# GpSimd's selection masks ahead of its wait for the tiny loads, P.V of quad 5 among the keys of quad 7, the first 24 heads turned ahead of the last maxima

## The chip, the cores and the metric

The kernel runs on one core of a Trainium2 chip. The metric is the device time of one launch in microseconds (us). Before the change the median of three runs is 202.33 us (201.74 to 202.46).

Five engines work beside each other, each with a queue of its own that is worked off in order: TensorE (PE in the profile; PEld is its weight load), VectorE (DVE), ScalarE (ACT), GpSimd (POOL) and SyncE (SP, which here only issues transfers). They meet at semaphores: an engine that reaches a wait stands until the count is there, and all that is behind it in its queue stands too.

## The reference

One token goes through two branches that are mixed by a gate. Cut to what matters:

```python
q = (x @ wq).reshape(32 heads, 128)
scores = q . k_cache * 128**-0.5          # 32 heads x 4096 keys x 128
p = softmax(scores)
a = (p . v_cache).reshape(4096) @ wo      # wo: 4096 x 512
h = relu(x @ w1 + b1); b = (h * h) @ w2 + b2
g = sigmoid(sum(x * gate_w))
out = g * a + (1 - g) * b                 # 512 values
```

The two caches are 32 MB each in bf16; with the weights the core reads some 78 MB.

## The kernel before

**Quads.** The 32 heads are worked through in 8 quads of 4 (`R = 4`, `NQ = 8`). The keys of a quad are 4 MB, laid as 128 partitions (4 heads x 32 rows) by 128 blocks of 128 elements; the values likewise. The SBUF tensor `KV` has four slots of 4 MB. SP issues the loads in the order K0, K1, V0, K2, V1, K3, V2, K4, V3, K5, V4, K6, K7, V5, V6, V7; from the fifth on, a load waits until what was in its slot is used up (`done`: for keys the products of DVE, `s_sd`, and the transposes of PE, `s_t`; for values `s_pv`). V7 comes in four parts of 1 MB. Behind V7 SP issues, once the last keys are used up, the last rows of `wo` (`wob`, L322, into the slot of K7) and most of `w2` (L307, L309).

**Scores.** Of the 128 blocks of a quad DVE takes 64 (16 in each quarter): one `tensor_tensor_reduce` a block (`ttr`, L702), which multiplies keys by the broadcast query `qb` and sums into a column of `S`. PE takes the other 64 in 8 groups of 8: it transposes a group (`transposes`, L480), ACT copies it from PSUM to `kT` (`evac`, L404), and PE multiplies it by the query column (`scores`, L492). In PE's queue the scores of a group stand two groups behind its transposes. After the eighth group ACT copies the scores to `S` (`s_copy`, L410).

**Softmax of a quad, done while the keys of the next one pass.** DVE takes the maximum over `S` (`smax`, L710, column of `mp`); PE turns it to a row (`max_rows`, L502) behind group 2 of the next quad; DVE reduces it to the four heads (`gmax`, L714 and L717, the row `dg`), behind the first 16 products of that quad; PE spreads it over the partitions (`max_cols`, L506) behind group 4; ACT copies it (`nM`, L414) and takes the exponentials with their sums (`exps`, L422) behind its fifth copy of a group. PE then sums over partitions (`den`, L514), multiplies by the values (`pv`, L525, 128 small matmuls), and DVE divides (`recip`, L724; `norm`, L730, which writes `onorm` and applies the gate). For quads 0 to 4 `den` and `pv` come at the end of the next quad's keys. Those of quad 5 come behind the last scores of quad 7, and after them the end of the kernel.

**The end.** PE's queue after the last scores: `den(5)`, `pv(5)`, `max_rows(7)`, `turn_a` (transposes `onorm` of heads 0 to 23, L545), `max_cols(7)`, `spread_a` (L552), `out_a` (L563, 128 matmuls with the rows of `wo` for the first 23 heads and more), `den(6)`, `pv(6)`, part of `w2`, `den(7)`, `pv(7)`, `regroup` for the last 8 heads (L569, L572), `out_b` (L581), the rest of `w2`, and the output.

**The selection masks.** `spread_a` puts the 24 heads' results into the order in which the rows of `wo` lie in SBUF, by a matmul with a 0/1 matrix (`selA`); `regroup` does so with `selB`. GpSimd makes both in the memory of `w1_sb`, once `mlp_h` (the first MLP matmuls, behind quad 2) has read `w1`: one memset (L363), one `affine_select` for `selB` (L365) and 19 for `selA` (L371, a count on `s_sb` after each, and each waits for the one before). Ahead of this GpSimd issues 14 transfers of rows of `wo` (L356) and 9 tiny transfers into unused memory (L353), which move the order of its DMA rings on; it waits for those 9 (L361, `s_dm`), then for `mlp_h` (`s_h`), and then makes the masks.

Of the kernel before, what the change touches and what calls it, by code (L numbers as in the profile page):

```python
# [5 lines left out]
def bass_gated_mix__gqa_block_cached__dense_activation_squared_relu__decode_kernel(  # L6
# [31 lines left out]
    R = 4  # L38
    NQ = NH // R
# [73 lines left out]
    with ctx:  # L113
# [90 lines left out]
        s_dm = [sem(f"s_dm{n}") for n in range(len(RUNS))]  # L204
# [22 lines left out]
        s_cp = sem("s_cp")  # L227
# [5 lines left out]
        s_nm = sem("s_nm")  # L233
# [3 lines left out]
        s_rd = sem("s_rd")  # L237
# [94 lines left out]
        @block.gpsimd  # L332
        def _(eng):
            eng.memset(ident[:, :], 0.0).then_inc(s_id, 1)
            eng.memset(identf[:, :], 0.0).then_inc(s_id, 1)
            eng.memset(onesf[:, :], 1.0).then_inc(s_cst, 1)
            eng.wait_ge(s_id, 2)
            for m in (ident, identf):
                eng.affine_select(out=m[:, :], in_=m[:, :], compare_op=ALU.not_equal, fill=1.0,
                                  base=0, pattern=[[-1, 128]], channel_multiplier=1)\  # L340
                   .then_inc(s_id, 1)
            eng.memset(E[:, :, :, :], 0.0).then_inc(s_ze, 1)
            eng.memset(RS[:, :], 0.0).then_inc(s_ze, 1)
            eng.memset(hd[:, :, :], 0.0).then_inc(s_ze, 1)
            eng.wait_ge(s_qps, NQ)
            q = 0
            sent = 0
            for n, ((back, d), run) in enumerate(zip(turns(), RUNS)):
                if back:
                    eng.inc_swdge_sem([], [], mode="reset_dge_cursor")  # L350
                if d:
                    src = B_w1[0:d, 0:32].rearrange("p (a c) -> p a c", a=2)
                    eng.dma_start(dm[0:d, sent, :, 0:8], src[:, :, 0:8]).then_inc(s_dm[sent], 16)  # L353
                    sent += 1
                p, st, k = place(*run)
                eng.dma_start(W[p:p + st * (k - 1) + 1:st, :], woa_v[q:q + k, :],  # L356
                              max_dma_last_dim=8192).then_inc(s_wp[n], 16)
                q += k
            assert q == STRIPS[len(RUNS)][3] and STRIPS[-1][3] + STRIPS[-1][2] == 4 * HX
            for n in range(sent):  # L360
                eng.wait_ge(s_dm[n], 16)  # L361
            eng.wait_ge(s_h, 1)
            eng.memset(w1_sb[0:NA, 0:3, 0:1024], 0.0).then_inc(s_sb, 1)  # L363
            eng.wait_ge(s_sb, 1)
            eng.affine_select(out=selB, in_=selB, compare_op=ALU.not_equal, fill=1.0,  # L365
                              base=0, pattern=[[8, 2], [1, 8], [-1, 128]], channel_multiplier=16)\
               .then_inc(s_sb, 1)
            for n, (p, st, k, q) in enumerate(STRIPS):
                eng.wait_ge(s_sb, n + 2)
                part = selA[:, :, p:p + st * (k - 1) + 1]  # L370
                eng.affine_select(out=part, in_=part, compare_op=ALU.not_equal, fill=1.0, base=-st * q,  # L371
                                  pattern=[[st, 4], [-1, st * (k - 1) + 1]], channel_multiplier=4 * st)\
                   .then_inc(s_sb, 1)

# [71 lines left out]
        def _(eng):  # L448
# [34 lines left out]
            def scores(q, g):  # L483
                n = GQ * q + g
                if g == 0:
                    eng.wait_ge(s_qc, q + 1)
                    if q >= 2:
                        eng.wait_ge(s_cp, R * (q - 1))
                eng.wait_ge(s_ev, n + 1)
                for y in range(GB):  # L490
                    c = GB * g + y
                    mm = eng.matmul(pS[q % 2][:, R * c:R * c + R], kT[:, n % NT, y * 128:(y + 1) * 128],  # L492
                                    qcol[:, R * q:R * q + R], start=True, stop=True)
                mm.then_inc(s_s2, 1)

            def max_rows(q):
                eng.wait_ge(s_mp, q + 1)
                if q >= 1:
                    eng.wait_ge(s_nm, q)
                if q >= 1:  # L500
                    eng.wait_ge(s_rd, q if q < NQ - 2 else q - 1)
                eng.transpose(MT, mp[:, q:q + 1], identf[:, :]).then_inc(s_mt, 1)  # L502

            def max_cols(q):
                eng.wait_ge(s_dg, q + 1)
                eng.matmul(MB[:, q:q + 1], dg[:, q % 2, :], onesf[0:1, 0:1],  # L506
                           start=True, stop=True).then_inc(s_mb, 1)

            def den(q):
                eng.wait_ge(s_e, R * (q + 1))  # L510
                eng.wait_ge(s_nm, q + 1 if q < NQ - 3 else min(q + 2, NQ))
                if q == NQ - 1:
                    eng.wait_ge(s_rd, q)
                eng.matmul(DEN[:, R * q:R * q + R], onesf[:, :], RS[:, R * q:R * q + R],  # L514
                           start=True, stop=True).then_inc(s_den, 1)

            def pv(q):
                if q >= 1:
                    eng.wait_ge(s_on, q)
                else:  # L520
                    eng.wait_ge(s_bg, 1)
                for j in range(NP):
                    eng.wait_ge(s_v[q][part_of(V_PARTS[q], j)], 16)
                    for b in range(PB * j, PB * j + PB):
                        mm = eng.matmul(O[:, R * q:R * q + R], KV[:, V_SLOT[q], b * 128:(b + 1) * 128],  # L525
                                        E[:, q % NE, COLUMN[b], :], start=(b == 0), stop=(b == NB - 1))
                mm.then_inc(s_pv, 1)
# [14 lines left out]
            def turn_a():  # L542
                eng.wait_ge(s_on, NA // R)
                eng.wait_ge(s_ev, GQ * NQ)
                eng.transpose(KP[2][0:NA, 0:128], onorm[:, 0:NA], ident[:, :]).then_inc(s_at, 1)  # L545

            def spread_a():
                eng.wait_ge(s_ac, 1)
                eng.wait_ge(s_cp, R * NQ)
                eng.wait_ge(s_sb, 2 + len(STRIPS))  # L550
                for c in range(4):
                    mm = eng.matmul(O2A, selA[:, c, :], oA[:, 32 * c:32 * c + 32],  # L552
                                    start=(c == 0), stop=(c == 3))
                mm.then_inc(s_at, 1)
# [63 lines left out]
            for q in range(NQ):  # L618
                for g in range(GQ):
                    transposes(q, g)  # L620
                    if g >= 2:
                        scores(q, g - 2)
                    for c, (a, b) in Q_AT.items():
                        if (a, b) == (q, g):
                            q_rows(c)
                        if (a, b + 2) == (q, g):
                            q_cols(c)
                    if g == 2 and q >= 1:
                        max_rows(q - 1)
                    if g == 4 and q >= 1:  # L630
                        max_cols(q - 1)
                scores(q, GQ - 2)
                scores(q, GQ - 1)
                if q == 0:
                    eng.wait_ge(s_b, 32)
                    eng.wait_ge(s_ez, 1)
                    eng.transpose(B2, b2r, ident[0:4, 0:4]).then_inc(s_b2, 1)
                if 1 <= q < NQ - 2:
                    den(q - 1)
                    pv(q - 1)  # L640
                if q == 2:
                    mlp_h()
            den(NQ - 3)
            pv(NQ - 3)
            max_rows(NQ - 1)
            turn_a()
            max_cols(NQ - 1)
            spread_a()
            eng.wait_ge(s_hs, 2)
# [19 lines left out]
        def _(eng):  # L669
# [82 lines left out]
            for q in range(NQ):  # L752
                for j in range(NP):
                    ttr(q, j)
                    if j == 0 and q == 1:
                        bias()
                    if j == 0 and q >= 1:
                        gmax(q - 1)
                    if j == 1 and 2 <= q < NQ - 1:
                        norm(q - 2)  # L760
                    if j == 1 and q == 4:
                        mlp()
                if q == NQ - 1:
                    recip(q - 2)
                    norm(q - 2)
                smax(q)
                if 1 <= q < NQ - 2:
                    recip(q - 1)
            gmax(NQ - 1)
            eng.wait_ge(s_at, 1)  # L770
            eng.tensor_copy(oA[:, :], KP[2][0:NA, 0:128]).then_inc(s_ac, 1)
            eng.wait_ge(s_at, 2)
            eng.tensor_copy(o2A[:, :], O2A).then_inc(s_ac, 1)
            for q in (NQ - 2, NQ - 1):
# [42 lines left out]
```

## Time and profile before

| | us |
|---|---|
| median of 3 runs | 202.33 (201.74 to 202.46) |
| the profiled execution | 202.62 |
| its span, first to last instruction | 201.3 |
| PE busy | 124.3 |
| DVE busy | 124.0 |
| ACT busy | 98.9 |
| GpSimd (POOL) busy | 37.7 |
| HBM read, 78.32 MB, over the span | 389 GB/s |
| mean granted PE clock | 0.674 of full |

In the page's 40 slices the DMA engines are busy at 9 tenths or more from the second slice to the 37th, and nearly idle in the last three. Busy times are shares of the whole span: an engine that waits for keys in the middle may still be the one that everything waits for at the end. Lines such as L525 are those of the kernel before.

### The profile page before, as it was taken

The page shows a single profiled execution, that of the slowest core. Times are in us where ns is not written, and L with a number is a line of the kernel's source. Part 1 is how long each engine was busy: PE and PEld are TensorE (multiplying, and loading weights), DVE is VectorE, ACT ScalarE, POOL GpSimd, SP SyncE. Part 2 cuts the span into 40 slices and gives each one's busy share as a digit, 9 for nine tenths or more (in the row PEclk, how much of TensorE's full clock was granted, in tenths as well). Part 3 has the DMA queues.
Part 4 walks back from the last instruction along what each step waited for, and adds up shares of the span by engine and source line. Part 5 has one row for each costly group of instructions (what it writes and reads, how often), then busy time and mean ns, then how long its engine had stood idle before and what let it go on. Part 6 is the DMA issues. An engine that isn't in the chain of part 4 may idle for free.

```text
span 201.3 us, 6499 instructions
## 1 busy us (share of the span) xinstructions
PE 124.3 (62%) x2420; PEld 111.2 (55%) x2422; DVE 124.0 (62%) x1086; ACT 98.9 (49%) x212; POOL 37.7 (19%) x56
## 2 busy tenths in 40 slices
PE   0039576982639298857279455925492825839686
PEld 0013365762639297846179355925492725829685
DVE  1100599999239950899079925993499999820011
ACT  3007489898119910695058803980298908340000
POOL 5000000069900000000000000000001979960000
PEclk9999799695557955695555555795579765555555
DMA  6999999999999999999999999999999999999300
GB/s 241 483 423 417 417 425 433 462 395 445 402 433 410 427 445 425 445 420 405 435 420 420 440 438 415 420 427 422 432 423 422 430 427 401 408 418 392 100 3 3
DMA packets 5659, 78.74 MB, mean 391 GB/s; under 512 B 1705, under 2 KB 2187, under 8 KB 2444
## 3 DMA queue, kind: packets, MB, share of 16 engines
q1 hardware_dynamic: 4078, 75.76, 88.7%
q0 software_dynamic: 1536, 2.56, 3.4%
q8 instruction: 19, 0.31, 0.6%
q14 instruction: 12, 0.10, 0.1%
q10 hardware_dynamic: 14, 0.01, 0.0%
HBM read 78.32 MB, written 0.00 MB: 389 GB/s over the span
## 4 chain that ended last, share of the span: by engine, by line
another core or an unknown queue 49%; POOL 17%; PE 11%; DMA 11%; ACT 5%; issue 4%; DVE 1%; POOLq 1%; SPq 0%; DVEq 0%; ACTq 0%
DMA KV<-in_A_k_cache_dram 11%; POOL w_sb L371 9%; POOL W L356 4%; PE pO L525 3%; ACT kT L404 3%; POOL xb L353 3%; PE pQ L462 3%; PE pQ L563 2%; ACT qb L393 2%; POOL w_sb L363 1%; POOL w_sb L365 1%; PE KP L480 1%; PE pQ L581 1%; PE pQ L597 0%
## 5 line engine op out<-in xcount | busy, mean ns | idle before, releaser
L702 DVE CUSTOM_DVE_ANT_0 KV<-KV,qb 128x128 bf16<-128x128 bf16 x512 | 113.1, 285 | 32.8 <-DMA KV<-in_A_k_cache_dram 32.8
L404 ACT ACTIVATE kT<-KP 128x1024 bf16<-128x1024 bf16 x64 | 62.1, 1026 | 55.3 <-PE KP L480 54.0
L480 PE MATMUL KP<-ident,KV 128*128 128x128 bf16 x512 | 51.8, 271 | 21.1 <-DMA KV<-in_A_k_cache_dram 21.1
L480 PEld LDWEIGHTS KP<-ident,KV 128*128 128x128 bf16 x512 | 42.9, 124 | 23.7 <-DMA KV<-in_A_k_cache_dram 20.1
L492 PE MATMUL pS<-qcol,kT 128*128 128x4 bf16 x512 | 23.6, 168 | 26.9 <-ACT kT L404 26.5
L702 DVE DVE_READ_ACCUMULATOR2_ANT S<- 128x1 f32 x512 | 38.4, 75 | 0.0
L492 PEld LDWEIGHTS pS<-qcol,kT 128*128 128x128 bf16 x512 | 21.0, 104 | 29.7 <-ACT kT L404 29.3
L525 PEld LDWEIGHTS pO<-E,KV 128*128 128x128 bf16 x1024 | 29.5, 105 | 1.8 <-issue 1.8
L525 PE MATMUL pO<-E,KV 128*128 128x4 bf16 x1024 | 28.6, 166 | 1.7 <-issue 1.7
L363 POOL MEMSET w_sb<- 24x3072 bf16 x1 | 2.6, 2647 | 100.0 <-DMA xb<-in_B_w_dram 100.0
L422 ACT ACTIVATE E<-S,nM 32x128 bf16<-32x128 f32 x32 | 18.4, 575 | 0.9
L371 POOL TENSOR_SCALAR_AFFINE_SELECT w_sb<-w_sb 24x36 bf16<-24x36 bf16 (+5 forms) x19 | 17.3, 910 | 3.1 <-POOL w_sb L371 0.5
L462 PE MATMUL pQ<-W,xb 128*128 128x512 bf16 x18 | 7.1, 530 | 12.3 <-DMA W<-in_A_wq_dram 10.9
L353 POOL DMA_DIRECT2D xb<-in_B_w_dram x9 | 5.3, 590 | 38.8 <-PE pQ L462 38.8
L393 ACT ACTIVATE qb<-pQ 32x128 bf16<-32x128 f32 x20 | 5.4, 268 | 13.0 <-PE pQ L462 12.6
L462 PEld LDWEIGHTS pQ<-W,xb 128*128 128x128 bf16 x20 | 2.0, 117 | 14.3 <-DMA W<-in_A_wq_dram 10.9
L410 ACT ACTIVATE S<-pS 32x64 f32<-32x64 f32 x32 | 6.9, 215 | 4.3 <-PE pS L492 3.7
L683 DVE TENSOR_SCALAR e<-ez 128x1 f32<-128x1 f32 x1 | 0.2, 154 | 12.8 <-ACT ez L431 12.8
L422 ACT ACTIVATION_READ_ACCUMULATOR E<-S,nM 32x1 f32 x32 | 8.0, 249 | 0.0
L356 POOL DMA_DIRECT2D W<-in_A_wo_dram x14 | 7.8, 562 | 0.0
L730 DVE SCALAR_TENSOR_TENSOR onorm<-pO,gcol,rden 128x4 bf16<-128x4 f32 x8 | 1.7, 211 | 9.8 <-PE pO L525 9.8
L506 PE MATMUL pM<-onesf,dg 1*128 1x1 f32 x16 | 3.6, 294 | 5.3 <-DVE dg L717 5.3
(86 smaller groups left out, 78.5 us busy)
## 6 DMA issues: line engine op xcount, KB each, us to landing
KV<-in_A_k_cache_dram SPq DMA_DIRECT2D x8, 4096.0 KB, 28.2
KV<-in_A_v_cache_dram SPq DMA_DIRECT2D x7, 4096.0 KB, 37.0
W<-in_A_wq_dram SPq DMA_DIRECT2D x1, 4096.0 KB, 12.5
KV<-in_A_v_cache_dram SPq DMA_DIRECT2D x4, 1024.0 KB, 21.8
W<-in_A_wo_dram POOLq DMA_DIRECT2D x2, 768.0 KB, 26.5
w_sb<-in_B_w_dram SPq DMA_DIRECT2D x1, 1376.0 KB, 11.6
w2a<-in_B_w_dram SPq DMA_DIRECT2D x2, 512.0 KB, 23.5
KV<-in_A_wo_dram SPq DMA_DIRECT2D x1, 1024.0 KB, 11.3
```

The source lines that it names most:

```text
L353: eng.dma_start(dm[0:d, sent, :, 0:8], src[:, :, 0:8]).then_inc(s_dm[sent], 16)
L356: eng.dma_start(W[p:p + st * (k - 1) + 1:st, :], woa_v[q:q + k, :], max_dma_last_dim=8192).then_inc(s_wp[n], 16)
L371: eng.affine_select(out=part, in_=part, compare_op=ALU.not_equal, fill=1.0, base=-st * q, pattern=[[st, 4], [-1, st * (k - 1) + 1]], chann ...
L393: eng.activation(qb[rows(r), c, :], QR[c][rows(r), r * 128:(r + 1) * 128], ACT.Copy)\
L404: eng.activation(kT[:, n % NT, :], KP[n % 3][:, :], ACT.Copy).then_inc(s_ev, 1)
L410: eng.activation(S[rows(r), q % NS, 0:YQ], S2[rows(r), :, r], ACT.Copy).then_inc(s_cp, 1)
L422: eng.activation(E[rows(r), q % NE, :, r], S[rows(r), q % NS, :], ACT.Exp, bias=nM[rows(r), q:q + 1], scale=SCALE, accum_out=RS[rows(r), h ...
L462: mm = eng.matmul(QR[c], xb[:, t, :], wq_sb[:, t, c * 512:(c + 1) * 512], start=(t == 0), stop=(t == 3))
L480: mm = eng.transpose(KP[n % 3][:, y * 128:(y + 1) * 128], key(q, b), ident[:, :])
L492: mm = eng.matmul(pS[q % 2][:, R * c:R * c + R], kT[:, n % NT, y * 128:(y + 1) * 128], qcol[:, R * q:R * q + R], start=True, stop=True)
L525: mm = eng.matmul(O[:, R * q:R * q + R], KV[:, V_SLOT[q], b * 128:(b + 1) * 128], E[:, q % NE, COLUMN[b], :], start=(b == 0), stop=(b == N ...
L702: ins = eng.tensor_tensor_reduce(key(q, b), key(q, b), qb[:, q, :], 1.0, 0.0, ALU.mult, ALU.add, S[:, q % NS, c:c + 1])
```

## The change

GpSimd's waits for the 9 tiny transfers move behind the masks. `den(5)` moves to the end of quad 6's keys, `pv(5)` behind group 4 and `max_cols(6)` of quad 7's keys; DVE's `recip(5)` follows `smax(6)`, and `norm(5)` follows the third quarter of quad 7's products. `turn_a` comes right behind the last scores, ahead of `max_rows(7)`; DVE's copy `oA` comes ahead of `gmax(7)`. Some waits are adapted: `max_rows(6)` now waits for `recip(5)`; `den(5)` no longer waits for `nM` of quad 6; `spread_a` waits for the score copies of quads 0 to 6 in place of all eight.

```diff
--- before.py
+++ after.py
@@ -357,8 +357,6 @@
             assert q == STRIPS[len(RUNS)][3] and STRIPS[-1][3] + STRIPS[-1][2] == 4 * HX
-            for n in range(sent):
-                eng.wait_ge(s_dm[n], 16)
             eng.wait_ge(s_h, 1)
             eng.memset(w1_sb[0:NA, 0:3, 0:1024], 0.0).then_inc(s_sb, 1)
             eng.wait_ge(s_sb, 1)
@@ -371,6 +369,8 @@
                                   pattern=[[st, 4], [-1, st * (k - 1) + 1]], channel_multiplier=4 * st)\
                    .then_inc(s_sb, 1)
+            for n in range(sent):
+                eng.wait_ge(s_dm[n], 16)
@@ -498,7 +498,7 @@  (max_rows)
                 if q >= 1:
-                    eng.wait_ge(s_rd, q if q < NQ - 2 else q - 1)
+                    eng.wait_ge(s_rd, q if q < NQ - 1 else q - 1)
@@ -508,7 +508,7 @@
             def den(q):
                 eng.wait_ge(s_e, R * (q + 1))
-                eng.wait_ge(s_nm, q + 1 if q < NQ - 3 else min(q + 2, NQ))
+                eng.wait_ge(s_nm, q + 1 if q < NQ - 2 else min(q + 2, NQ))
@@ -546,7 +546,7 @@
             def spread_a():
                 eng.wait_ge(s_ac, 1)
-                eng.wait_ge(s_cp, R * NQ)
+                eng.wait_ge(s_cp, R * (NQ - 1))
@@ -629,21 +629,22 @@
                     if g == 4 and q >= 1:
                         max_cols(q - 1)
+                    if g == 4 and q == NQ - 1:
+                        pv(q - 2)
                 scores(q, GQ - 2)
                 scores(q, GQ - 1)
...
+                if 1 <= q < NQ - 1:
+                    den(q - 1)
                 if 1 <= q < NQ - 2:
-                    den(q - 1)
                     pv(q - 1)
                 if q == 2:
                     mlp_h()
-            den(NQ - 3)
-            pv(NQ - 3)
+            turn_a()
             max_rows(NQ - 1)
-            turn_a()
             max_cols(NQ - 1)
             spread_a()
@@ -760,15 +761,14 @@
                     if j == 1 and q == 4:
                         mlp()
-                if q == NQ - 1:
-                    recip(q - 2)
-                    norm(q - 2)
+                    if j == 2 and q == NQ - 1:
+                        norm(q - 2)
                 smax(q)
-                if 1 <= q < NQ - 2:
+                if 1 <= q < NQ - 1:
                     recip(q - 1)
-            gmax(NQ - 1)
             eng.wait_ge(s_at, 1)
             eng.tensor_copy(oA[:, :], KP[2][0:NA, 0:128]).then_inc(s_ac, 1)
+            gmax(NQ - 1)
             eng.wait_ge(s_at, 2)
             eng.tensor_copy(o2A[:, :], O2A).then_inc(s_ac, 1)
```

## The prediction

> **What bounds the kernel now.** I read the chain of work that ended last first, then the waits, the timelines of PE and DVE from 155 us on, the landings of the loads, and the DMA queues.
>
> The chain from 155 us runs through GpSimd's mask building and then through PE alone (columns: start us, us, what).
>
> ```profile
> 155.11 2.66 POOL w_sb L363
> ...
> 165.06 10.16 POOL w_sb L371
> ...
> 179.67 0.24 POOL w_sb L371
> ...
> 180.42 0.28 PE pS L552 x4
> 180.72 0.20 DVE o2A L773
> ...
> 181.29 3.55 PE pQ L563 x128
> 184.84 0.43 PE pM L514 x2
> 185.27 0.69 PE pO L525 x26
> 185.96 1.75 issue
> 187.71 2.88 PE pO L525 x102
> 190.59 0.43 PE pQ L597 x16
> 191.02 0.43 PE pM L514 x2
> 191.44 3.45 PE pO L525 x128
> ```
>
> So from 180.42 to the end the span is PE's own queue, and `spread_a` (L552) starts when the last mask is there. The waits say how long each side stood (total us, times, longest us).
>
> ```profile
> POOL w_sb L363 <- DMA xb<-in_B_w_dram: 100.0, 1, 100.0
> ...
> PE pS L552 <- POOL w_sb L371: 1.9, 1, 1.9
> ```
>
> In the timeline PE, in quad 7, first stands for DVE's `dg` (`max_cols(6)`), and after P.V of quad 5 for `mp` of the last quad.
>
> ```profile
> 164.99 0.58 PE L506 MATMUL pM<-onesf,dg 1*128 1x1 f32 x2 [4.91 <-DVE dg L717]
> 165.50 1.03 PE L480 MATMUL KP<-ident,KV 128*128 128x128 bf16 x8
> ...
> 176.96 0.37 PE L502 MATMUL pM<-identf,mp 128*1 128x128 f32 x1 [0.57 <-DVE mp L710]
> ```
>
> DVE's time in quad 7 in two stretches (stretch, length, busy and records; then clock, DMA share, GB/s): 16 key products beside GpSimd, then 48 products and two small operations while GpSimd stood in one 10.16 us instruction.
>
> ```profile
> 158.03:164.41 6.38, 6.38 (x32) 0.77 0.99 420
> 164.41:175.10 10.69, 10.66 (x101) 0.50 0.96 405
> ```
>
> The second stretch gives 0.2125 us a product. DMA: the values of quad 5 were issued at 137.2 and took 25.8 us.
>
> ```profile
> L278 SPq DMA_DIRECT2D KV<-in_A_v_cache_dram x1: 328/328/328, 137.2 to 137.2; - x1
> ...
> DMA to landing us min/median/max: 25.8/25.8/25.8
> ```
>
> They land at 163.0. The same answer for the other large loads gives K6 143.5, K7 153.2, V6 172.7, V7's four parts 176.4 to 183.9, and for the last weights 186.5 (`wob`) to 189.0.
>
> **The 1.75 us of "issue"** is PE without instructions. Queue 8 carries 19 packets of 0.31 MB in all, 16 KB or 256 instructions of 64 bytes each (an estimate from PE's 4955 records of all kinds). The halts at 77.20 and 187.71 lie a multiple of 256 records apart. A packet of the next-but-one block starts 2.1 to 4.7 us (mean 3.2) after PE crosses a block's end while the load queue is full, 1.1 once it is empty. It lasts 1.07 and is usable some 1.4 later (186.30 to 187.71). A loaded block thus takes 5.6 us, while 128 small matmuls with their weight loads use one up in 3.6. The window from crossing to halt's end, and the code packet in 185 to 186.5 and in 188.7 to 190.1:
>
> ```profile
> 182.04:187.70 5.66, 3.92 (x134) 3.84 (x130) 0.18 (x1) 0.00 (x0) 0.00 (x0) 0.50 0.95 355
> ...
> q8 instruction: 1, 0.02, 4.9%
> ...
> q8 instruction: 1, 0.02, 5.4%
> ```
>
> **The change, part by part.**
>
> *Masks before the wait.* GpSimd now waits only for `mlp_h` (L538's last matmul, 80.3), so its 24.9 us (155.1 to 180.0) start near 80.5, beside quads 3 and 4. Price there: in quad 7 the contact cost DVE 6.38 - 16 x 0.2125 = 3.0 us, and GpSimd then stood still until DVE ended. Take 3 us late in quad 3 and 1 in quad 4 (bounds 0, if GpSimd falls into DVE's gap, and 14.7, all its 24.9 us less the 10.2 in which it stood). DVE's gap before the next keys is 5.84 us (95.9 to 101.7). SP's issues behind it (K5 at 95.44, V4 at 96.67) may slip by 15 us, for K4 and V3 fill the queue until 113.2. Cost 0; without that queue, one for one.
>
> *The same in quad 7.* DVE gets 3.0 us back: `dg` of quad 6 at 158.03 + 0.17 (`recip(5)`, moved to here) + 3.40 + 0.31 = 161.9, `max_cols(6)` at 162.2 instead of 164.99. `den(5)` moves ahead of quad 7: 0.43 us on PE at 155.5, in front of a 4.91 us wait. `recip(5)` needs it, and `max_rows(6)` now needs `recip(5)`: 0.2 us, in the same slack.
>
> *P.V of quad 5 after `max_cols(6)`.* PE waits for the values until 163.0; 128 x 27.7 ns (row: 3.55) ends at 166.6. Behind it stand the transposes of groups 5 to 7, the scores, and on ACT `exps(6)` and the last copy. They started at 165.50 and now start at 166.65, 1.15 later. From there to the end of ACT's `s_copy(7)` the row is 8.0 us (165.50 to 173.51): 174.65. DVE is free by 158.2 + 64 x 0.2125 + 0.46 + `norm(5)` 0.2 = 172.5 (`norm(5)` finds P.V done). So `mp(7)` starts at 174.7, where it was 176.63: 1.95 earlier. SP's `wob`, behind the last product, is issued 2.6 us sooner, into a queue full until 183.9: 0.
>
> *`turn_a` ahead, `oA` ahead of `gmax(7)`.* 0.28 us on PE and 0.20 on DVE, both beside the wait for `mp(7)`: 0; if exposed, 0.5 together.
>
> *`spread_a`.* From `mp` to `max_cols(7)` stays 1.32 us, and the mask wait of 1.9 goes. Sum so far 1.95 + 1.9 = 3.85, taken as 3.9: `out_a` at 177.4. What is late next is code. PE crosses a block's end 0.75 us into `out_a` (178.15), needs the block 4.67 us after `out_a`'s start (182.05), and has it at 178.15 + 5.6 = 183.75: the same halt, 1.7. The next crossing then lies at 187.55 (before: 187.71 to 191.49, 3.78). Its block was requested at 183.75. With a drained queue that is 1.1 + 1.2 + 1.4 = 3.7 us, halt 0; with a loaded one 5.6, halt 1.8. Before, that request fell at 187.71, when loads were over. At 184 to 187 the DMA share is still 0.97 to 0.92, but in small packets (240 in the last microsecond, against 64 at 182). I take 0.8, near the middle, and keep both ends. So that crossing is at 188.3 instead of 191.49, and all that follows (`wob` 186.5, weights 189.0) is in before PE asks. End 201.3 - 3.2 = 198.1.
>
> [...]
>
> The profiled execution took 202.62, 1.32 beside its span; 202.62 - 3.2 = 199.4. It lay 0.29 over the median of the runs, 202.33: **199.1**.
>
> **Rivals.**
>
> 1. *My sum*, second halt 0 to 1.8: 198.3 to 200.2. Chance 0.60.
> 2. *Code always comes in time:* nothing after `out_a` halts. 202.33 - 3.9 - 1.75 = 196.7. For it: P.V of quads 1 to 4 (128 matmuls in 3.55) never halted; against: they followed slow stretches. Chance 0.06. [...]
> 3. *The inserted P.V eats its gain:* the values or PE's next block come 2 us late (that block is asked for near 159.6, usable near 165.2, needed at 166.0), quad 7's rest ends as late as before, and only the mask wait goes: 202.33 - 1.9 = 200.4, with a part of the second halt, 0.3, 200.7 (200.2 to 201.3). Against: loads land 9.7 to 11.5 us apart in strict order. Chance 0.18.
> 4. *PE starves to the end:* the third block is also fetched under load, 3.9 - 1.8 - 1.8 gives 202.0, no change. Against: the queue is empty by 189. Chance 0.07.
> 5. *Slower:* masks beside DVE in quads 3 and 4 hold the key slots so long that the load queue runs dry. It decides once quad 3 ends over 15 us late (113.2); from there 1 us for 1 us, and past the 3.2 us gain slower: 203.5 to 206. For it: one mask instruction took 10.16 us; against: there GpSimd stood, not DVE. Chance 0.09.
>
> **Numbers.** A measurement of this kernel tells about 0.5% from no change (201.3 to 203.3). Faster: 0.60 + 0.06 + 0.18 = 0.84; same 0.07; slower 0.09. The range holds cases 1 and 3 (0.78) and, for half a microsecond that any landing may shift, a little beyond both: 197.5 to 201.5. The likeliest case's own range is 198.3 to 200.2.
>
> **What the new profile would show.** Masks (L363 to L371, shifted) near 80 to 120 us; first key product of quad 7 at 0.28, not 2.04; P.V of quad 5 near 163, after `dg` near 162; `mp(7)` near 174.7; no wait of `spread_a` for GpSimd; `out_a` near 177.4; "issue" in P.V of quad 6 near 1.7 and again early in P.V of quad 7. I am wrong if P.V of quad 5 starts after 164.5, if the halts add to more than 3.6 or less than 1.7, or if a key load in quads 4 to 6 lands late.

## The result, and the profile after

The changed kernel takes 200.54 us (median of six runs, 200.07 to 201.13) against 202.60 for the kernel before in the same comparison. The ratio is 0.990, with a 95% interval of 0.9871 to 0.9929: faster by about 1.0%, where 1.6% was forecast. The profiled execution took 200.49, its span is 199.1, from unrounded spans 2.1 under the span before.

The chain that ended last in the changed kernel, its last part (columns: start us, us, what):

```profile
173.27 0.39 PE pS L492 x8
...
174.64 0.30 DVE mp L711
174.99 0.39 PE pM L502
...
175.98 0.58 PE pM L506 x2
176.56 0.14 PE pS L552 x4
...
177.02 3.55 PE pQ L563 x128
...
181.69 1.42 issue
183.11 2.88 PE pO L525 x102
...
187.03 2.33 issue
189.36 3.40 PE pO L525 x121
```

GpSimd has left this part of the chain. `mp` of the last quad comes at 174.64 (before: 176.63), `spread_a` follows `max_cols` at once, and `out_a` (L563) starts at 177.02 (before: 181.29), 4.27 earlier. Half of this does not reach the end: PE stands for code once more, for 2.33 us after seven matmuls of P.V of quad 7, at a place where the kernel before ran through.

The masks in GpSimd's timeline of the changed kernel, and PE around P.V of quad 5:

```profile
81.21 2.65 POOL L361 MEMSET w_sb<- 24x3072 bf16 x1 [26.37 <-PE pQ L538]
...
86.16 19.52 POOL L369 TENSOR_SCALAR_AFFINE_SELECT w_sb<-w_sb 24x188 bf16<-24x188 bf16 x19
```
```profile
162.03 0.38 PE L506 MATMUL pM<-onesf,dg 1*128 1x1 f32 x2 [1.15 <-DVE dg L718]
163.00 3.76 PE L525 MATMUL pO<-E,KV 128*128 128x4 bf16 x128 [0.60 <-DMA KV<-in_A_v_cache_dram]
166.62 1.01 PE L480 MATMUL KP<-ident,KV 128*128 128x128 bf16 x8
```

The masks are made from 81.2 to 105.7, beside quads 3 and 4. In quad 7 `max_cols(6)` comes at 162.03 instead of 164.99, and P.V of quad 5 then waits 0.60 for its values. DVE's first 16 products of quad 7 take 3.38 us where they took 6.38 (stretch, length; busy and records of PE, PEld, DVE, ACT and POOL; clock, DMA share, GB/s):

```profile
158.07:161.45 3.38, 2.80 (x52) 2.65 (x50) 3.38 (x34) 3.38 (x5) 0.00 (x0) 0.80 0.99 419
```

Quad 3 bore the masks: its first product beside a select takes 2.14 us at 84.02, K5 is issued at 97.56 instead of 95.44, and lands 25.6 us later, at 123.2, where it landed at 122.8.

### The profile page after: what moved, and what is told of

Read it like the earlier page. It is cut to its first block, busy times and chain, and to the rows that moved or that the text cites. A ratio compares the mean times of both kernels' runs of the same rounds, so it can differ in the third digit from the quotient of the medians.

```text
span 199.1 us, 6499 instructions
## 1 busy us (share of the span) xinstructions
PE 122.8 (62%) x2420; PEld 111.3 (56%) x2422; DVE 123.7 (62%) x1086; ACT 98.7 (50%) x212; POOL 37.3 (19%) x56
## 4 chain that ended last, share of the span: by engine, by line
DMA 52%; DVE 30%; PE 12%; issue 3%; ACT 2%; SPq 0%; DVEq 0%
DMA KV<-in_A_k_cache_dram 39%; DVE KV L703 27%; DMA KV<-in_A_v_cache_dram 13%; PE pO L525 5%; PE pQ L563 2%; PE KP L480 1%; DVE S L703 1%; ACT kT L404 1%; ACT E L422 1%; PE pQ L581 1%; PE pQ L597 0%; PE pO L606 0%; DVE gm L715 0%; DVE dg L718 0%; ACT S L410 0%
## 5 line engine op out<-in xcount | busy, mean ns | idle before, releaser
L480 PE MATMUL KP<-ident,KV 128*128 128x128 bf16 x512 | 52.5, 273 | 21.6 <-DMA KV<-in_A_k_cache_dram 21.5
L480 PEld LDWEIGHTS KP<-ident,KV 128*128 128x128 bf16 x512 | 43.5, 126 | 23.9 <-DMA KV<-in_A_k_cache_dram 19.7
L462 PE MATMUL pQ<-W,xb 128*128 128x512 bf16 x18 | 6.6, 499 | 11.9 <-DMA W<-in_A_wq_dram 10.7
```

The costliest lines, as they stand in the source:

```text
L462: mm = eng.matmul(QR[c], xb[:, t, :], wq_sb[:, t, c * 512:(c + 1) * 512], start=(t == 0), stop=(t == 3))
L480: mm = eng.transpose(KP[n % 3][:, y * 128:(y + 1) * 128], key(q, b), ident[:, :])
```

## The experiments

All ratios are to the kernel before, run beside each kernel on the same chip. The changed kernel again, run beside two of the kernels further down (60 matmuls more, and P.V of quad 6 early):

> The changed kernel once more, beside the other two on the same chip: 0.987 to 0.993 of before by either theory; its halts again after 26 matmuls of P.V of quad 6 and 7 of P.V of quad 7.

200.59 us, 0.9907 (0.9889 to 0.9926), halts of 1.27 and 2.33 after 26 and 7 matmuls: the result repeats.

### Which part carries the gain

**Masks alone.** The kernel before, with this edit only:

```diff
-            for n in range(sent):
-                eng.wait_ge(s_dm[n], 16)
             eng.wait_ge(s_h, 1)
...
+            for n in range(sent):
+                eng.wait_ge(s_dm[n], 16)
```

> The kernel before with one edit: GpSimd's waits for the tiny loads stand behind the masks; PE's and DVE's order is as before. Theory A (nearly all of the gain is the masks: DVE freed of GpSimd in quad 7, and no wait of spread_a; the move of P.V of quad 5 adds nothing, since the same 128 matmuls lie ahead of the last maximum in either order and here they need not wait for the values): dg of quad 6 at 162.0, scores of quad 7 done near 169.5, P.V of quad 5 170 to 173.6, mp of quad 7 at 174.0, out_a near 176.4; time 0.985 to 0.992 of before, 199.5 to 201. Rival B (the move of P.V of quad 5 earns its part): mp of quad 7 no earlier than 176, out_a at 178.5 or later; time 0.995 or more of before.

**The moves on PE and DVE alone.** The changed kernel with the reverse of this edit:

> The changed kernel with GpSimd's waits put back ahead of the masks: all moves on PE and DVE, no earlier masks. Theory A (the masks carry the gain): DVE again shares with GpSimd, dg of quad 6 near 164.5, P.V of quad 5 165 to 169, mp of quad 7 near 177, spread_a again behind the last mask at 180 to 180.5, the end as before: 0.997 to 1.006 of before. Rival B (the moves of P.V and of the turn earn 2 us by themselves): 0.990 of before.

Masks alone: 200.17 us, 0.9881 (0.9854 to 0.9908). The moves alone: 202.07 us, 0.9978 (0.9964 to 0.9992). PE's timeline with the masks alone:

```profile
170.15 3.55 PE L525 MATMUL pO<-E,KV 128*128 128x4 bf16 x128
174.28 0.37 PE L502 MATMUL pM<-identf,mp 128*1 128x128 f32 x1 [0.57 <-DVE mp L710]
...
176.31 3.55 PE L563 MATMUL pQ<-o2A,W 128*128 128x1 bf16 x128 [0.33 <-DVE o2A L773]
...
182.80 2.88 PE L525 MATMUL pO<-E,KV 128*128 128x4 bf16 x102 [1.82 <-issue]
...
189.05 3.39 PE L525 MATMUL pO<-E,KV 128*128 128x4 bf16 x121 [2.33 <-issue]
```

The whole gain of this change is there without any move of P.V. The same 128 matmuls lie ahead of the last maximum in either order; here they run at 170.15 without a wait, `out_a` starts 0.7 us earlier than in the changed kernel, and the first halt is 0.4 longer. The two kernels cannot be told apart by their intervals. With the moves alone, `spread_a` again stands behind the last mask (180.15) and almost all of the gain is gone.

**What the masks' place does: two halves.** The changed kernel, in which GpSimd does the same memset and selects a second time, on unused memory, at the old place:

```diff
             for n in range(sent):
                 eng.wait_ge(s_dm[n], 16)
+            k0 = 2 + len(STRIPS)
+            eng.memset(w1_sb[32:32 + NA, 0:3, 0:1024], 0.0).then_inc(s_sb, 1)
...
+            for n, (p, st, k, q) in enumerate(STRIPS):
+                eng.wait_ge(s_sb, k0 + n + 2)
+                part = xA[:, :, p:p + st * (k - 1) + 1]
+                eng.affine_select(out=part, in_=part, compare_op=ALU.not_equal, fill=1.0, base=-st * q,
+                                  pattern=[[st, 4], [-1, st * (k - 1) + 1]], channel_multiplier=4 * st)\
+                   .then_inc(s_sb, 1)
```

> The changed kernel, in which GpSimd, after its masks and its wait for the tiny loads (near 155 us), does the same memset and the same 20 selects once more on memory that nobody reads. The masks that spread_a needs are there early; only the company of DVE in the first products of quad 7 is as before the change. Theory A (the company costs DVE 3.0 us, and half of the earlier start of out_a comes from its end): dg of quad 6 near 164.4, mp of quad 7 near 176.8, no wait of spread_a for GpSimd, out_a near 179.2, half-way between 177.0 and 181.3; time 0.994 to 0.999 of before. Rival F (the company is slack, only the wait for the masks counted): mp of quad 7 near 174.7, out_a near 177, time as the changed kernel, 0.990.

201.09 us, 0.9937 (0.9916 to 0.9957), a little under the band named. The positions are those of theory A. DVE's first product of quad 7 takes 2.04 us again (first line), and PE's timeline has the rest:

```profile
157.94 2.04 DVE L717 CUSTOM_DVE_ANT_0 KV<-KV,qb 128x128 bf16<-128x128 bf16 x1
```
```profile
164.91 0.58 PE L520 MATMUL pM<-onesf,dg 1*128 1x1 f32 x2 [4.77 <-DVE dg L732]
...
179.26 3.55 PE L577 MATMUL pQ<-o2A,W 128*128 128x1 bf16 x128 [0.33 <-DVE o2A L787]
...
185.48 2.88 PE L539 MATMUL pO<-E,KV 128*128 128x4 bf16 x102 [1.55 <-issue]
...
189.80 3.39 PE L539 MATMUL pO<-E,KV 128*128 128x4 bf16 x121 [0.41 <-issue]
```

So GpSimd's company costs 2.24 us at `out_a` (179.26 against 177.02). At the end it costs only 0.5: the kernel that is later at `out_a` has halts of 1.55 and 0.41, 1.96 in all, against 1.42 and 2.33, 3.75.

### The halts

A halt here is a stop of PE in the middle of a run of matmuls, with no releaser but "issue". In the prediction's reading PE's code comes in blocks of 256 records, and the block after the next is asked for when PE enters the next one. In the trace of the changed kernel the halts that end at 77.87, 183.11 and 189.36 lie 2816 (11 x 256) and 256 records apart. "Asked for" below is that moment, worked out from the trace; the trace does not record the request itself, only the packet that brings the block.

**Every block's end moved.** The changed kernel with 44 small matmuls more at its start, while PE waits for `wq`:

```diff
+            for _ in range(44):
+                eng.matmul(pQ[:, 0:4], ident[:, :], ident[:, 0:4], start=True, stop=True)
             eng.wait_ge(s_wq, 16)
```

> The changed kernel with 44 more small matmuls (88 PE records) into unused PSUM at its start, while PE waits for wq. Theory C (the halts are ends of 256-record code blocks): every block ends 88 records earlier. The halt after 26 matmuls of P.V of quad 6 goes, the end of that block now falling in out_a's last matmuls, where its block has had 6 us; one halt of 1.8 to 2.4 after some 116 matmuls of P.V of quad 6; none, or under 0.3, in P.V of quad 7. Sum of halts near 2 in place of 3.75, the end 1.5 to 2 earlier: 0.980 to 0.984 of before, 198.5 to 199.2. Rival D (the halts belong to these places: values, PSUM or a semaphore in P.V): still after 26 and 7 matmuls, 3.75 in all, time as the changed kernel, 0.99.

201.24 us, 0.9921 (0.9894 to 0.9948): not the gain that theory C named. But the halts moved:

```profile
177.04 3.15 PE L565 MATMUL pQ<-o2A,W 128*128 128x1 bf16 x113 [0.40 <-DVE o2A L775]
181.96 0.56 PE L565 MATMUL pQ<-o2A,W 128*128 128x1 bf16 x15 [1.77 <-issue]
...
182.81 3.07 PE L527 MATMUL pO<-E,KV 128*128 128x4 bf16 x110
188.35 0.64 PE L527 MATMUL pO<-E,KV 128*128 128x4 bf16 x18 [2.47 <-issue]
```

The first moved from behind 26 matmuls of P.V of quad 6 to behind 113 of `out_a`, the second from behind 7 of P.V of quad 7 to behind 110 of quad 6. Counted back from the last record of PE, the second halt lies 500 records from the end, where it lay 412: 88 earlier, as many as were added. The halts belong to the code's blocks and not to values, PSUM or a semaphore at these places; rival D is out. What failed in my expectation is that the first would vanish: its packet came 6.1 us after the block's end that precedes it (173.4 to 179.45). Over the blocks that PE leaves up to 182 us, while loads run, in all the kernels here, this delay is 1.7 to 7.0 us, but for one of 0.3 and one of 7.9, both early in this run; what makes it long in one case and short in another I have not settled. This run also has a halt of 2.46 at 56.58, in P.V of quad 1, where PE has to wait for keys behind it anyway.

**Without the loads.** The changed kernel without the load of V7 (P.V of quad 7 reads what its slot held before):

```diff
-                load_kv(n)
+                if n < len(ORDER) - 1:
+                    load_kv(n)
...
-                    eng.wait_ge(s_v[q][part_of(V_PARTS[q], j)], 16)
+                    if q < NQ - 1:
+                        eng.wait_ge(s_v[q][part_of(V_PARTS[q], j)], 16)
```

> The changed kernel without the load of the values of quad 7 (4 MB): its P.V reads what its slot held before, so the output is not the reference's. The load queue is then empty near 179, not 188. Theory C (a code block is late because its packet stands behind the loads): no halt over 0.5 us in P.V of quads 6 and 7, span near 195.5. Rival E (the block's fetch takes 5.6 us with or without loads): both halts stay, 1.4 and 2.3, span near 199.

One run: 196.48 us, span 195.1. The queue is empty by 180 (the first row, 180 to 185 us, ends in 3 GB/s), and PE's timeline has the other two:

```profile
180.00:185.00 5.00, 4.83 (x160) 4.74 (x157) 0.41 (x2) 0.00 (x0) 0.00 (x0) 0.50 0.02 3
```
```profile
181.59 2.88 PE L527 MATMUL pO<-E,KV 128*128 128x4 bf16 x102 [0.17 <-issue]
...
185.18 3.55 PE L527 MATMUL pO<-E,KV 128*128 128x4 bf16 x128
```

Halts of 0.17 and none, in place of 1.42 and 2.33, with `out_a` at 176.74. So it is the loads that make a block late. The run takes all of them away at that point; whether the packet stands in line behind them or they slow it in another way it does not tell.

**Another place for the blocks.** As above, with 60 in place of 44:

> The changed kernel with 60 small matmuls (120 PE records) at its start, where the run with 44 had them. Theory C, with the request going out at the block's end or up to some 30 records behind it: this block's end now lies ahead of the last scores of quad 7 (near 169.8 us), more than 30 records ahead of the wait for mp, so the next block is there by 179; its end falls after some 100 matmuls of out_a (179.9): no halt there. One halt of 1.5 to 2.5 us after some 100 matmuls of P.V of quad 6, at most 0.5 in P.V of quad 7. Span 197 to 197.7, 0.979 to 0.984 of before. If the halts only move and add up to 3.7 or more again, as with 44, a block's end costs the same wherever it falls in the tail, and the span is 199 or more.

199.22 us, 0.9840 (0.9821 to 0.9858). No halt in `out_a`; 1.29 after 94 matmuls of P.V of quad 6, and then, against the expectation, 1.80 after 75 of P.V of quad 7: that block was asked for at 184.47, and its packet moved at 187.6. The sum is 3.1 instead of 3.75, and the time 1.4 us better than that of the changed kernel beside it. The halts do not account for all of that: its profiled execution is only 0.7 us better (199.53 against 200.21), and the mean granted PE clock was 0.580 in it, against 0.688. The places of the blocks change what the halts cost; none of the three tried does away with the second halt (2.33, 2.47 and 1.80) while loads run to 188.

### What to do with it

**P.V of quad 6 into the waits.** The changed kernel, with

```diff
             turn_a()
+            pv(NQ - 2)
             max_rows(NQ - 1)
-            max_cols(NQ - 1)
             spread_a()
+            max_cols(NQ - 1)
             eng.wait_ge(s_hs, 2)
             out_a()
             den(NQ - 2)
-            pv(NQ - 2)
```

> The changed kernel with P.V of quad 6 right behind turn_a, ahead of max_rows(7), and spread_a between max_rows(7) and max_cols(7). Theory C (late code costs only where PE has nothing to wait for; a block takes 5 to 6 us under load, so its request has to go out early): P.V of quad 6 runs 174.0 to 177.6 inside the time in which PE waited for mp, dg and o2A; out_a near 179.4 with a halt under 1 us, one halt of 1 to 2 us early in P.V of quad 7, which ends near 189.6 in place of 192.7. Span near 196, 0.972 to 0.980 of before. Rival D (the tail is bound by something that the order does not touch, such as the last weights at 189): P.V of quad 7 ends after 191.5, 0.986 or more.

197.40 us, 0.9746 (0.9726 to 0.9766): faster than both kernels, and where theory C put it.

```profile
173.63 3.57 PE L525 MATMUL pO<-E,KV 128*128 128x4 bf16 x128
...
178.91 0.88 PE L563 MATMUL pQ<-o2A,W 128*128 128x1 bf16 x28 [0.27 <-issue]
180.42 2.81 PE L563 MATMUL pQ<-o2A,W 128*128 128x1 bf16 x100 [0.63 <-issue]
...
186.64 3.39 PE L525 MATMUL pO<-E,KV 128*128 128x4 bf16 x121 [1.86 <-issue]
```

P.V of quad 6 runs while DVE and PE pass the last maximum to and fro, and the code block behind it is asked for at 174.72 instead of 177.77. The 0.27 us ahead of `out_a` are no block's end and are not counted as a halt for code.

**The same with P.V of quad 5 left at its old place:**

> The kernel before with the masks early, turn_a and oA ahead, and P.V of quad 6 ahead of max_rows(7), but with P.V of quad 5 left behind the last scores. Theory A (the place of P.V of quad 5 is worth nothing): P.V of quad 5 170.1 to 173.6, P.V of quad 6 from 174.1, out_a near 179, 0.973 to 0.979 of before, within 0.4 us of the run with both P.V moved. Rival B (it earns its part once the tail is dense): 0.982 or more.

199.61 us, 0.9865 (0.9843 to 0.9886). Here theory A, that the place of P.V of quad 5 is worth nothing, falls, and rival B holds:

```profile
169.77 3.55 PE L525 MATMUL pO<-E,KV 128*128 128x4 bf16 x128
173.70 0.28 PE L545 MATMUL KP<-ident,onorm 128*24 128x128 bf16 x1 [0.38 <-DVE onorm L730]
...
176.56 2.49 PE L525 MATMUL pO<-E,KV 128*128 128x4 bf16 x88 [1.42 <-issue]
...
182.84 2.81 PE L563 MATMUL pQ<-o2A,W 128*128 128x1 bf16 x100 [1.20 <-issue]
...
189.05 3.39 PE L525 MATMUL pO<-E,KV 128*128 128x4 bf16 x121 [1.86 <-issue]
```

Two P.V in a row use up two blocks in 7 us, while the three of this tail took 5.7 to 6.3 to come; a halt of 1.42 is added and one of 0.63 grows to 1.20. With P.V of quad 5 at 163, its block is fetched while ACT and PE work through the slow groups of quad 7: in the changed kernel a block's end falls at 166.06, the packet asked for there moves from 169.60 to 170.62, and its block is needed only at 177.77.

The tail of all kernels but the repeat, from PE's timelines (us; the span is that of the profiled execution, the ratio is the one given above):

| kernel | `out_a` starts | halts for code in the tail | span | ratio |
|---|---|---|---|---|
| before | 181.29 | 1.75 | 201.3 | 1 |
| moves alone | 181.05 | 1.55 | 200.8 | 0.998 |
| GpSimd's work repeated | 179.26 | 1.55, 0.41 | 199.6 | 0.994 |
| 44 matmuls more | 177.04 | 1.77, 2.47 | 199.6 | 0.992 |
| changed | 177.02 | 1.42, 2.33 | 199.1 | 0.990 |
| masks alone | 176.31 | 1.82, 2.33 | 198.8 | 0.988 |
| P.V 6 early, P.V 5 late | 180.75 | 1.42, 1.20, 1.86 | 198.8 | 0.987 |
| 60 matmuls more | 176.70 | 1.29, 1.80 | 198.2 | 0.984 |
| P.V 6 early | 178.91 | 0.63, 1.86 | 196.4 | 0.975 |
| without V7 | 176.74 | 0.17 | 195.1 | one run |

## Why the prediction was right, and where its size was off

*Masks early:* right in place, and near in price. They ran from 81.2 to 105.7; by SP's next issues quad 3 ended 2.1 us later and quad 4 1.0, where 3 and 1 were allowed. In the other runs with early masks quad 3 ended 3.1 to 4.8 later, so the price of 3 was on the low side, but far from the 15 us at which it would have counted. The loads' landings show that nothing downstream noticed: K5 came 0.4 us later, V4 0.2, K6, K7 and V5 within 0.1.

*DVE in quad 7:* right. 3.0 us came back, `max_cols(6)` at 162.03 (forecast 162.2). That the masks' company was the cause is shown by the run that repeats GpSimd's work: DVE's first product of quad 7 takes 2.04 us in it, 0.26 in the changed kernel, and `max_cols(6)` comes at 164.91.

*P.V of quad 5, `mp(7)`:* 163.00 and 174.64, forecast 163.0 and 174.7. I gave the whole 1.95 us to masks and move together, and did not work out the change without the move. The run with the masks alone has the maximum another 0.7 us earlier: the move brought nothing in this kernel.

*`spread_a` and `out_a`:* forecast 177.4, measured 177.02; the sum of 3.9 was 4.27.

*The first halt:* forecast 1.7, measured 1.42.

*The second halt* is the term that was mis-sized: "I take 0.8, near the middle, and keep both ends." It measured 2.33, over the upper end of 1.8 too. The block was asked for at 183.11, its packet began only at 186.88, 3.8 us later, and PE had the block at 189.36, 6.25 after the request, where 5.6 was the loaded price. The middle was chosen because the last loads move in small packets (before: 240 in the microsecond from 186, 64 in that from 182). Requests that went out later, in other runs, show where that holds: 3.2 us to the packet at 184.47 (60 matmuls more), 2.0 at 185.47 (GpSimd's work repeated, whose second halt was 0.41), 1.1 to 1.2 at 187.27 and 187.71 (moves alone, before). So the later requests in the last loads waited less, but those at 183.11 and 184.47, with 3.8 and 3.2, still paid the loaded price (3.2 to the packet in the mean). The prediction's own row pointed to that end: the request was forecast for 183.75, and the DMA share was still 0.97 in the microsecond from 184. With it (a halt of 1.8) the sum would have been 200.4 for the profiled execution, which took 200.49. In all: 4.27 + 0.33 (first halt shorter) - 2.33 = 2.27, and the span is 2.1 shorter.

*The range, and the signs of being wrong.* The time lies in the range stated, but 0.3 above the likeliest case's own, in the stretch that was put in for rival 3 (200.2 to 201.3), whose mechanism did not happen. That the range held is so in part luck: the chain of steps was right, one of its terms was outside its own bounds. Of the three signs named, one came: the halts add to 3.75, more than 3.6 (3.60 in the repeat). P.V of quad 5 did not start after 164.5, and no key load in quads 4 to 6 landed more than 0.4 late.

*Rivals.* Code that always comes in time (196.7) is what the run without V7 looks like, and only that. That P.V eats its gain, and that masks dry the load queue, did not happen. The starving tail came half true: one more halt of the full size, not two.

## What to carry to other kernels

When an edit brings a dense stretch of small instructions forward, ask where its code comes from: 256 PE records were used up in 3.6 us, and those that PE halted for in the tails had taken 5.2 to 6.4 us to come while loads ran (one 4.3, one 8.6), so the gain of an earlier start can be paid back in part in halts for "issue" (here 4.27 us at `out_a`, 2.1 at the end). Such stretches did best here apart from one another, in places where PE waited for something else: P.V of quads 5 and 6 each in such a place gave 0.975, one right behind the other 0.987. And where a change has several parts, work out the sum for each one without the others: here one of them carried all of the gain, and another was worth nothing until a third was added.

## What the runs showed of the hardware that was not expected

- A code packet that was asked for some 5 us before the loads ended still waited its full time: 3.8 us from 183.11 in the changed kernel, with loads until 188, against a mean of 3.2 in the full queue. Later requests waited less: 3.2 at 184.47, 2.0 at 185.47, 1.1 at 187.71, each in another kernel. The two in between are one request each.
- Adding 44 matmuls in an idle stretch at the start of a kernel moved both halts by 88 records. Adding 60 made the kernel 1.4 us (0.7%) faster than adding none; 0.5 to 0.7 us of that are shorter halts, and where the rest comes from is not shown.
